# Where the first softmax of the second batch starts: its maxima moved one weight step earlier, its exponentials half a block earlier

## The chip, the cores and the metric

The kernel runs on one core of one Trainium2 chip. The metric is the device time of one execution in microseconds (us), lower is better. PE is TensorE (matrix products), DVE is VectorE, ACT is ScalarE, POOL is GpSimd, and SP issues the loads and stores.

## The reference, cut to what matters

Attention with two kinds of mask (four heads see the last 32 positions, four see every 32nd position) over 2 batches of 576 tokens, then a gated product of two linear layers with two more linear layers behind it, then four experts that are mixed by given probabilities.

```python
scores = scale * np.matmul(q, k.transpose(0, 1, 3, 2))      # B, H, S, D = 2, 8, 576, 64
scores = np.where(masks, scores, -1e9)
scores = scores - np.max(scores, axis=-1, keepdims=True)
attn = np.exp(scores); attn = attn / (np.sum(attn, axis=-1, keepdims=True) + 1e-09)
x = np.matmul(attn, v)                                       # to (1152, 512)
a = x @ w1; b = x @ w2; h = a * b @ w3; x = h @ w_out        # d_ff = 1024
for e in range(4):
    out += p[:, e:e + 1] * (np.maximum(x @ w1e[e], 0.0) @ w2e[e])
```

## The kernel before

Every matrix product with weights is made of three products of a value split in a high and a low part (`mm3`, lines 303 to 307). The weights arrive as 64-bit numbers and are turned into such pairs on the chip by a **worker**, a generator (`work`, lines 260 to 291). `advance(1)` makes its next step. For one chunk of weights the steps are `clamp` (DVE, L185), `shift` (DVE, L188), `round_up` and `sign` (ACT L144, DVE L191), then `magnitude` of the next chunk with `add` of this one (ACT L149, DVE L195), and, when the next chunk has begun, the split in the high part (ACT, L203) and the low part (DVE, L232). Product block `ft` needs both parts of chunk `ft`.

The order of all work is written out by hand: every engine runs its own instructions strictly in the order in which the program issues them. From line 1044 on, `run_unit` issues one **unit** after another: unit number `done` covers one `ft` and one half (288 tokens) of a batch. A unit has two half blocks of twelve matmuls each. The first ends in a copy of the accumulator by ACT (L609), the second in a product by DVE (L611) that reads the second accumulator and that copy. After each half block comes one step of the worker. Units 0 and 1 are made ahead of the loop, so the loop begins with unit 2.

Between the units the attention of the second batch is threaded in by `attend(1, s)`. Batch 1 has six chunks of scores. `attend` with s = 0 to 8 issues, among other things, the row maxima of chunk s (`maxima`: DVE reduction L409, then POOL multiplies the maxima by the negative scale, L411), the normalisation of chunk s-1 (POOL L436 adds a constant to the sums, DVE L453 takes reciprocals, DVE L457 multiplies), the transposes of chunk s-2 (PE, L462) and, from s = 2 on, the scores of chunk s+1 (PE, L396 and L403). The scores of chunks 0 to 2 are made ahead of the loop (line 1035). The exponentials of chunk s (`slots_exps`: ACT, L433, six or eight of them, one for each slot, each with its sum) are not issued by `attend`; it puts the chunk on the list `waiting`, and `run_unit` issues them at the end of the next half block, behind the worker's step there.

So before the change `attend(1, 0)` stands behind unit 3, `attend(1, 1)` behind unit 4 and `attend(1, 2)` behind unit 5. The exponentials of chunk 0 are issued at the end of the first half block of unit 4.

Of the kernel before, what the change touches and what calls it, by code (L numbers as in the profile page):

```python
# [44 lines left out]
def kernel(  # L45
# [249 lines left out]
    def advance(n=1):  # L295

        return all([next(worker, False) for _ in range(n)])

    def need(c, part=0):
        while not (c.done if part == 0 else c.done1 if part == 1 else c.done2):  # L300
            assert advance()
# [284 lines left out]
    def ab_block(b, ft, n):  # L586
        t = slice(b * S + n * HB, b * S + n * HB + HB)
        pair, late = ft // 2, b == 0 and ft < 6
        ab = tmp.tile([P, HB], F32, tag="pT", name="ab")
        if n == 0 and ft % 2 == 0:  # L590
            if late:
                if pair < 2:
                    parts = big[pair].tile([P, 2, 2, S], F32, tag="big", name="ab_f32")
                    whole[pair] = parts[:, 0]
                    if pair:
                        whole[2] = parts[:, 1]
            elif (b, pair) not in parts_of:
                ab_place(b, pair)
        if late:
            full = whole[pair][:, ft % 2, n * HB:n * HB + HB]  # L600
        else:
            full = ab
            pieces = ab_pieces(b, ft, n * HB, HB)
        for w in range(2):
            acc = bank("ab_acc")[:, :HB]
            for k in range(4):
                mm3(acc, c_w12[ft].parts((w * 4 + k) * P, P), (x_hi[:, k, t], x_lo[:, k, t]), k == 0, k == 3)
            if w == 0:
                nc.scalar.copy(ab, acc)  # L609
            else:  # L610
                nc.vector.tensor_tensor(out=full, in0=acc, in1=ab, op=ALU.mult)  # L611
            yield
        if late:
            return
        split_hi(pieces, ab)
        yield
        split_lo(pieces, ab)
        yield
# [241 lines left out]
    with tc.manual_schedule():  # L860
# [22 lines left out]
        done = 0  # L883
# [2 lines left out]

        waiting = []

        def run_unit():

            nonlocal done, rest
            b, ft, i = units[done]
            if done >= 2:
                need(c_w12[ft])
            block = ab_block(b, ft, i)
            for _ in range(2):
                next(rest, None)
                next(block)
                if done >= 2:
                    advance(1)  # L900
                if waiting:
                    waiting.pop().slots_exps()
            rest = block
            done += 1
            if b == i == 1:
                c_w12[ft].free()

        def attend(b, s):

            nonlocal live  # L910
            chunk = chunks[b]
            n = len(chunk)
            if 3 <= s + 1 < n:
                chunk[s + 1].scores()
            if s < n:
                chunk[s].maxima()
            if 1 <= s <= n:
                chunk[s - 1].recip()
                chunk[s - 1].normalise()
            if 3 <= s:  # L920
                c = chunk[s - 3]
                c.pv()
                c.put()
                c.put_lo()
                if c.g == 0:
                    live -= 1
            if 2 <= s < n + 2:
                chunk[s - 2].transposes()
                chunk[s - 2].evac(nc.scalar.copy)
            if s < n:  # L930
                waiting.append(chunk[s])
# [109 lines left out]
        done = 2  # L1041
        advance(4)
        steps = iter(range(9))
        while done < 16:
            if done == 3:
                need(c_w12[2])
            run_unit()
            if done in (4, 5, 6, 7, 8, 10, 11, 13, 14):
                attend(1, next(steps))
            if done == 6:  # L1050
                zero.whole_split()
        load_probs()
        while done < 32:
            run_unit()
            if done in (18, 21, 24):
                ab_split({18: 0, 21: 1, 24: 2}[done])
# [50 lines left out]
        for c in wc[:3]:  # L1107
# [6 lines left out]
        steps = [Step(half, e, c, c_e[16 * i + 4 * e + c])  # L1114
                 for i, half in enumerate(halves) for e in range(E) for c in range(4)]
# [100 lines left out]
```

## Time and profile before

| what | value |
|---|---|
| time, median of 3 runs | 616.2 us (616.09 to 616.81) |
| the profiled execution's own time | 618.54 us |
| its span, first to last instruction | 616.8 us |
| PE busy | 610.5 us (99%) |
| DVE busy | 442.1 us (72%) |
| ACT busy | 279.9 us (45%) |
| POOL busy | 16.2 us (3%) |
| mean granted TensorE clock | 0.997 |

The profiled execution took 618.54 us as a whole; its trace covers 616.8 us of that. A busy PE is one that has matmuls in flight. The share of an engine is a mean over stages of different kinds: the place of the change lies between 40 and 60 us, where DVE has much less room than its 72% say.

### The profile page before, as it was taken

The numbers are of one execution on the slowest core, as the hardware profiler recorded it, in microseconds if no ns is written. First come the engines' busy times: TensorE is split into PE (matmuls) and PEld (weight loads), VectorE is DVE, ScalarE is ACT, GpSimd is POOL, SyncE is SP. The second block draws the span as 40 slices with busy tenths as digits, with TensorE's granted clock in tenths as the row PEclk, the third lists the DMA queues.
The fourth block names the chain that finished last, engine by engine and source line by source line (L and its number), as shares of the span: only waits on it lengthen the run. The fifth ranks groups of instructions, "written<-read, shape, count | busy, mean of one in ns | idle before, by whom it ended". The sixth has DMA issues, their size and how long they took to land.

```text
span 616.8 us, 11164 instructions
## 1 busy us (share of the span) xinstructions
PE 610.5 (99%) x4488; PEld 557.0 (90%) x4488; DVE 442.1 (72%) x805; ACT 279.9 (45%) x562; POOL 16.2 (3%) x45
## 2 busy tenths in 40 slices
PE   8999999999999999999999999999999999999997
PEld 5789999998889999999899998999889898989996
DVE  4799977999753227777877987887766665755843
ACT  4769966776743134333343433434343333333320
POOL 4102200000000000000000000000000000000000
PEclk9899999999999999999999999999999999999999
DMA  8987340245412201333445344435585557464411
GB/s 264 319 299 210 135 143 2 82 157 201 176 68 94 85 28 69 137 138 136 192 158 193 121 158 168 167 144 205 184 324 196 214 193 249 162 234 175 153 53 69
DMA packets 28314, 99.48 MB, mean 161 GB/s; under 512 B 2630, under 2 KB 6158, under 8 KB 25830
## 3 DMA queue, kind: packets, MB, share of 16 engines
q1 hardware_dynamic: 27718, 98.17, 44.6%
q8 instruction: 35, 0.57, 0.4%
q10 hardware_dynamic: 544, 0.59, 0.3%
q14 instruction: 17, 0.14, 0.1%
HBM read 79.62 MB, written 19.14 MB: 160 GB/s over the span
## 4 chain that ended last, share of the span: by engine, by line
PE 98%; DMA 1%; issue 0%; ACT 0%; DVE 0%; ACTq 0%
PE g_acc L305 11%; PE g_acc L306 11%; PE g_acc L307 11%; PE ab_acc L305 5%; PE ab_acc L307 5%; PE ab_acc L306 5%; PE m_a L307 4%; PE m_a L306 4%; PE m_a L305 4%; PE m_b L306 3%; PE m_c L305 3%; PE m_b L305 3%; PE m_c L306 3%; PE x_acc L305 3%; PE m_c L307 3%; PE m_b L307 3%
## 5 line engine op out<-in xcount | busy, mean ns | idle before, releaser
L769 ACT ACTIVATE h_hi<-u 128x320 fp32r<-128x320 f32 (+1 forms) x128 | 56.9, 445 | 189.2 <-DVE u L775 189.2
L305 PE MATMUL g_acc<-w_hi,h_hi 128*128 128x512 f32 (+1 forms) x296 | 114.3, 386 | 0.0
L306 PE MATMUL g_acc<-w_lo,h_hi 128*128 128x512 f32 (+1 forms) x296 | 114.2, 386 | 0.0
L307 PE MATMUL g_acc<-w_hi,h_lo 128*128 128x512 f32 (+1 forms) x296 | 113.7, 384 | 0.0
L708 DVE TENSOR_TENSOR w_lo<-raw,w_hi 128x768 fp32r<-128x768 f32 x64 | 69.5, 1086 | 12.4 <-ACT w_hi L706 12.3
L775 DVE TENSOR_TENSOR u<-m_b,u 128x320 f32<-128x320 f32 (+1 forms) x96 | 40.8, 453 | 50.1 <-PE m_b L307 50.1
L305 PE MATMUL ab_acc<-x_hi,w_hi 128*128 128x288 f32 x240 | 71.4, 297 | 0.0
L307 PE MATMUL ab_acc<-x_hi,w_lo 128*128 128x288 f32 x240 | 70.7, 295 | 0.0
L306 PE MATMUL ab_acc<-x_lo,w_hi 128*128 128x288 f32 x240 | 70.7, 294 | 0.0
L307 PEld LDWEIGHTS g_acc<-w_hi,h_lo 128*128 128x128 f32 x296 | 55.6, 188 | 11.6
L305 PEld LDWEIGHTS g_acc<-w_hi,h_hi 128*128 128x128 f32 x296 | 55.8, 188 | 8.0
L306 PEld LDWEIGHTS g_acc<-w_lo,h_hi 128*128 128x128 f32 x296 | 55.8, 188 | 7.6
L771 DVE SCALAR_TENSOR_TENSOR h_lo<-u,h_hi 128x320 fp32r<-128x320 f32 (+1 forms) x128 | 57.9, 452 | 3.6 <-ACT h_hi L769 1.4
L706 ACT CAST w_hi<-raw 128x768 fp32r<-128x768 f32 x64 | 59.9, 936 | 0.0
L305 PEld LDWEIGHTS ab_acc<-x_hi,w_hi 128*128 128x128 f32 x240 | 45.0, 188 | 0.1
L306 PEld LDWEIGHTS ab_acc<-x_lo,w_hi 128*128 128x128 f32 x240 | 45.0, 188 | 0.0
L307 PEld LDWEIGHTS ab_acc<-x_hi,w_lo 128*128 128x128 f32 x240 | 45.0, 188 | 0.0
L306 PE MATMUL m_b<-b_t,s_hi 128*128 128x320 f32 (+1 forms) x128 | 37.9, 296 | 0.0
L775 DVE TENSOR_TENSOR u<-m_a,u 128x320 f32<-128x320 f32 (+1 forms) x64 | 28.9, 452 | 11.6 <-PE m_a L307 11.6
L708 DVE TENSOR_TENSOR s_lo<-raw,s_hi 128x1024 fp32r<-128x1024 f32 x16 | 19.6, 1226 | 24.3 <-ACT s_hi L706 24.3
L775 DVE TENSOR_TENSOR u<-m_c,u 128x320 f32<-128x320 f32 (+1 forms) x64 | 29.1, 454 | 4.5 <-PE m_c L307 3.9
L785 ACT COPY u<-m_a 128x320 f32<-128x320 f32 (+1 forms) x32 | 12.8, 399 | 42.1 <-PE m_a L307 42.1
(182 smaller groups left out, 1396.4 us busy)
## 6 DMA issues: line engine op xcount, KB each, us to landing
raw<-in_e_dram SPq DMA_DIRECT2D x32, 1024.0 KB, 4.9
raw<-in_w3T_dram SPq DMA_DIRECT2D x8, 1024.0 KB, 4.9
stored<-s_hi SPq DMA_DIRECT2D x16, 512.0 KB, 2.6
stored<-s_lo SPq DMA_DIRECT2D x16, 512.0 KB, 2.7
s_hi<-stored SPq DMA_DIRECT2D x16, 512.0 KB, 3.7
s_lo<-stored SPq DMA_DIRECT2D x16, 512.0 KB, 5.4
raw<-in_w_dram SPq DMA_DIRECT2D x7, 1024.0 KB, 7.8
raw<-in_w_out_dram SPq DMA_DIRECT2D x4, 1024.0 KB, 5.0
```

Of the source, the lines that this page charges most:

```text
L305: mm(acc, lh, rh, start=first, stop=False)
L306: mm(acc, lh, rl, start=False, stop=False)
L307: mm(acc, ll, rh, start=False, stop=last)
L706: nc.scalar.copy(dst[0], src)
L708: nc.vector.tensor_tensor(out=dst[1], in0=src, in1=dst[0].bitcast(F32), op=ALU.subtract)
L769: nc.scalar.activation(hi, src, AF.Relu)
L771: nc.vector.scalar_tensor_tensor(out=lo, in0=src, scalar=0.0, in1=hi.bitcast(F32), op0=ALU.max, op1=ALU.subtract)
L775: nc.vector.tensor_tensor(out=out, in0=acc, in1=b, op=ALU.add)
L785: nc.scalar.copy(u1, a)
```

## The change

`run_unit` takes a function that it calls in the second half block of the unit, behind the block's own instructions and ahead of the worker's step. It is given for unit 3 alone, and does `attend(1, 0)` there; the call behind unit 3 is gone. The list of the other eight calls is as it was.

```diff
-        def run_unit():
+        def run_unit(between=None):
...
-            for _ in range(2):
+            for i_half in range(2):
                 next(rest, None)
                 next(block)
+                if between and i_half:
+                    between()
                 if done >= 2:
                     advance(1)
                 if waiting:
...
+        def begin():
+            attend(1, next(steps))
+
         while done < 16:
             if done == 3:
                 need(c_w12[2])
-            run_unit()
-            if done in (4, 5, 6, 7, 8, 10, 11, 13, 14):
+            run_unit(begin if done == 3 else None)
+            if done in (5, 6, 7, 8, 10, 11, 13, 14):
                 attend(1, next(steps))
```

`attend(1, 0)` issues the maxima of chunk 0 and puts the chunk on `waiting`. Since the list is looked at behind the worker's step of the same half block, the exponentials move too.

On DVE, from the worker's `sign` step in unit 3 on, these rows stood before (`raw` and `t` are a chunk of weights, `ab_f_623` the products of units 2 and 3, `ab_f_831` those of unit 4, `mx` the maxima, `sc` the scores):

```order
L191 SCALAR_TENSOR_TENSOR t<-raw_611,t 128x1024
L611 TENSOR_TENSOR ab_f_623<-ab_acc,ab 128x288
L195 ISA t<-raw_611,t 128x2048
L409 TENSOR_REDUCE mx<-sc 128x6
L185 TENSOR_SCALAR t<-t 128x1024
L611 TENSOR_TENSOR ab_f_831<-ab_acc,ab 128x288
L232 TENSOR_TENSOR w_lo<-t,w_hi 128x1024
```

With the change the same place reads as follows (`ab_f_839` is the tile that was `ab_f_831`):

```order
L611 TENSOR_TENSOR ab_f_623<-ab_acc,ab 128x288
L409 TENSOR_REDUCE mx<-sc 128x6
L195 ISA t<-raw_611,t 128x2048
L185 TENSOR_SCALAR t<-t 128x1024
L611 TENSOR_TENSOR ab_f_839<-ab_acc,ab 128x288
```

The reduction L409 has changed places with the worker's addition L195; nothing else on DVE moved.

On ACT the difference between before (-) and the change (+) is this, from the worker's steps in unit 3 to those in unit 5 (the first L609 is the copy of unit 4, the second that of unit 5; `w_hi` is the high part of weight chunk 3; `p_ring` takes the exponentials):

```order
 L144 ACTIVATE raw_611<-raw_611 128x1024
 L149 ACTIVATE t<-raw_729 128x1024
-L609 COPY ab<-ab_acc 128x288
-L203 CAST w_hi<-t 128x1024
 L433 ACTIVATE p_ring,rec<-sc,mx 128x64 x6
+L609 COPY ab<-ab_acc 128x288
+L203 CAST w_hi<-t 128x1024
 L609 COPY ab<-ab_acc 128x288
 L144 ACTIVATE raw_729<-raw_729 128x1024
```

The six exponentials of chunk 0 now stand ahead of unit 4's copy and of the split of weight chunk 3. PE, POOL and SP issue the same instructions in the same order as before.

## Rows read from the trace of the kernel before

**Rows 1.** The page, part 1: engine, busy time, share of the span, instructions.

```profile
PE 610.5 (99%) x4488; PEld 557.0 (90%) x4488; DVE 442.1 (72%) x805; ACT 279.9 (45%) x562; POOL 16.2 (3%) x45
```

**Rows 2.** Waits of PE: us in total, times, longest us; first of four rows.

```profile
PE o L483 <- issue: 1.4, 1, 1.4
...
```

**Rows 3.** Timeline of PE, 49.5 to 51.3 us: start, duration, line, tiles, count.

```profile
49.51 0.34 PE L396 MATMUL sc<-m_str,i_str 128*128 128x432 bf16 x1
49.78 1.01 PE L403 MATMUL sc<-tqk 64*54 64x54 f32 x32
50.74 0.55 PE L462 MATMUL tp<-ident,p_ring 128*128 128x128 f32 x3
```

**Rows 4.** Timeline of DVE, 44.7 to 50.7 us.

```profile
44.77 0.45 DVE L611 TENSOR_TENSOR ab_f<-ab_acc,ab 128x288 f32<-128x288 f32 x1
45.14 1.22 DVE L195 CUSTOM_DVE_ANT_0 t<-raw,t 128x2048 uint16<-128x2048 uint16 x1
46.27 0.55 DVE L409 TENSOR_REDUCE mx<-sc 128x6 f32<-128x384 f32 x1
46.74 0.68 DVE L185 TENSOR_SCALAR t<-t 128x1024 f32<-128x1024 f32 x1
47.34 0.45 DVE L611 TENSOR_TENSOR ab_f<-ab_acc,ab 128x288 f32<-128x288 f32 x1
47.71 1.22 DVE L232 TENSOR_TENSOR w_lo<-t,w_hi 128x1024 fp32r<-128x1024 f32 x1
48.84 0.69 DVE L188 TENSOR_SCALAR t<-t 128x1024 int32<-128x1024 int32 x1
49.44 0.55 DVE L409 TENSOR_REDUCE mx<-sc 128x6 f32<-128x384 f32 x1
...
50.12 0.56 DVE L457 TENSOR_TENSOR p_ring<-p_ring,rec 128x384 f32<-128x384 f32 x1
```

**Rows 5.** Timeline of ACT, 43 to 50.9 us; in brackets the idle time before.

```profile
43.06 1.15 ACT L149 ACTIVATE t<-raw 128x1024 f32<-128x1024 f32 x1
44.89 0.40 ACT L609 COPY ab<-ab_acc 128x288 f32<-128x288 f32 x1 [0.68 <-PE ab_acc L307]
46.39 1.05 ACT L203 CAST w_hi<-t 128x1024 fp32r<-128x1024 f32 x1 [1.10 <-DVE t L195]
47.57 0.32 ACT L433 ACTIVATE p_ring<-sc,mx 128x64 f32<-128x64 f32 x1
...
49.33 0.42 ACT L609 COPY ab<-ab_acc 128x288 f32<-128x288 f32 x1
49.61 1.20 ACT L144 ACTIVATE raw<-raw 128x1024 int32<-128x1024 uint32 x1
```

**Rows 6.** Timeline of POOL, 46 to 59 us.

```profile
46.91 0.62 POOL L411 TENSOR_SCALAR mx<-mx 128x6 f32<-128x6 f32 x1 [27.01 <-DVE mx L409]
...
50.08 0.25 POOL L411 TENSOR_SCALAR mx<-mx 128x6 f32<-128x6 f32 x1 [0.21 <-DVE mx L409]
...
58.10 0.82 POOL L436 TENSOR_SCALAR rec<-rec 128x6 f32<-128x6 f32 x1 [3.99 <-ACT p_ring L433]
```

**Rows 7.** Timeline of DVE, 57 to 58.9 us, while that last POOL instruction ran.

```profile
57.05 1.22 DVE L232 TENSOR_TENSOR w_lo<-t,w_hi 128x1024 fp32r<-128x1024 f32 x1
58.19 0.69 DVE L188 TENSOR_SCALAR t<-t 128x1024 int32<-128x1024 int32 x1
```

**Rows 8.** Stretches: length, busy us and instructions by engine, granted clock (PEclk), DMA share, GB/s.

```profile
16.90:20.30 3.40, 2.01 (x88) 1.69 (x80) 2.62 (x7) 1.89 (x5) 2.09 (x6) 1.00 0.92 272
20.30:23.70 3.40, 3.40 (x56) 3.01 (x49) 1.46 (x3) 1.54 (x5) 0.00 (x0) 0.50 0.84 335
23.70:27.00 3.30, 3.19 (x74) 2.54 (x73) 2.58 (x5) 3.01 (x13) 0.00 (x0) 1.00 1.08 430
```

**Rows 9.** Timelines of SP and of ACT: a weight load, and the first reader of its data.

```profile
46.38 7.31 SPq L140 DMA_DIRECT2D raw<-in_w_dram  x2
...
62.07 1.37 ACT L149 ACTIVATE t<-raw 128x1024 f32<-128x1024 f32 x1
```

## The prediction, made before the change was run

> **What bounds the kernel now.** I read the page first: PE is busy for 610.5 of 616.8 us [rows 1]. A busy share can hide waits, so the waits of PE come next: there are four rows of them, 3.0 us in all, the longest 1.4 us [rows 2], and all lie in the first 20 us. Behind those PE waits for nothing the profile can show. That fixes what a change of order between 40 and 60 us can do: PE runs the same instructions in the same order, there is no wait to remove, so the time can only stay or grow by waits that are made new. The question is how much room each thing has that PE waits for.
>
> The timeline of PE shows where the room is smallest. Behind the matmuls of unit 5 come the scores of chunk 3 at 49.51 and 49.78, and at 50.74 the transposes of chunk 0 [rows 3]. The scores reuse the accumulator that the exponentials of chunk 0 read; the last of these is over shortly before the next ACT instruction at 49.33 [rows 5], so this one is met with almost no room, but it is met. The transposes need DVE's normalisation of chunk 0, which runs from 50.12 to 50.68 [rows 4]; the transposes start 0.06 us later [rows 3]. So **DVE may not be late here at all**: whatever it loses ahead of 50.12, PE loses at 50.74. Its rows from 44.77 on follow each other without a gap (none carries a wait) [rows 4]; DVE has no slack to lose it from.
>
> ACT, on the other hand, stands idle twice just there: 0.68 us ahead of unit 4's copy at 44.89 and 1.10 us ahead of the cast at 46.39 [rows 5]. The six exponentials take from 47.57 to 49.33, 1.76 us [rows 5]. They would just fill these two gaps, if their maxima were there in time.
>
> **When the maxima are there.** DVE's product of unit 3 starts at 44.77 and lets the next one start at 45.14 [rows 4]. So the reduction of chunk 0 starts at 45.14 instead of 46.27 and ends 0.55 us later, at 45.69. The addition L195 starts 0.47 us behind the reduction's start (before, L185 followed it so, 46.27 to 46.74 [rows 4]), at 45.61, and ends at 46.83. L185 follows 1.13 us behind it (45.14 to 46.27), at 46.74, as before, and ends at 47.42.
>
> The maxima then pass through POOL, which is not among the rows that moved but decides the case. Undisturbed its multiplication takes 0.25 us (at 50.08); at 46.91 it took 0.62 us and ended at 47.53, 0.11 us behind the end of DVE's L185 at 47.42 [rows 4, 6]. At 58.10 a POOL instruction of the same size began while DVE ran L232, which ended at 58.27; L188 had started at 58.19, ahead of that end, and POOL was done at 58.92, just behind L188's end at 58.88 [rows 6, 7]. So POOL is held by some DVE instructions, and when the next such one starts before the first has ended, it is held through both. That is the new case: POOL starts 0.09 us behind the reduction (46.91 less 46.82), at 45.78, when L195 already runs, and L195 runs into L185. Held through both it ends at about 47.5, where it ended before. The exponentials then start at 47.57 as before: **earlier in the order, not in time**. POOL has nothing else queued until the sums.
>
> The Trainium skill, "SBUF — State Buffer", section "SBUF: two separate sides", says that GpSimd and some VectorE instructions share a pair of ports as an exclusive lock, which whoever starts first has for its whole instruction. The holding at 46.91 agrees with it. It does not say who has the lock when POOL has waited through L195 and L185 started before that was over; if POOL has it, the sum is that of the second rival.
>
> **What is queued behind them now.** Before, ACT did unit 4's copy at 44.89 and the cast of weight chunk 3 at 46.39, ahead of the exponentials. Now both wait behind them, and DVE waits for both:
>
> - The exponentials end at 47.57 + 1.76 = 49.33. The copy follows, 49.33 to 49.75 (0.42, as the copy there took [rows 5]).
> - DVE's product of unit 4 needs the copy: it starts at 49.79 instead of 47.34 [rows 4].
> - The cast starts 0.28 us behind the copy (49.33 to 49.61 [rows 5]), at 49.61, takes 1.05 to 1.1, ends at about 50.68.
> - DVE's low part L232 needs the cast: it starts at 50.72 instead of 47.71. **DVE is 3.0 us late.**
> - The spacings stay: L188 1.13 behind L232, the reduction of chunk 1 at 0.60 behind that, the normalisation 0.68 behind that (47.71, 48.84, 49.44, 50.12 [rows 4]). It runs from 53.13 to 53.69, and the transposes start at 53.75 instead of 50.74.
>
> So PE stands still for **3.0 us**, behind its scores. The lower bound of this cost is with POOL not held at all (0.25 us): exponentials at 46.06, copy at 47.82, cast to 49.16, L232 at 49.20, 1.5 us late.
>
> Nothing else is lost by it. The weight load on SP that started at 46.38, right behind L195's end (46.36), now starts 0.47 us later; its data have their first reader at 62.07 [rows 9], over 8 us after the row's end. ACT's copy of unit 5 goes from 49.33 to about 50.6, late by less than PE. Behind the transposes PE, DVE and ACT are all late by 2.7 to 3.0 us, so no new wait follows; and as PE had no waits later, nothing gives the 3.0 us back. The gain is the 0.04 us at most by which the scores at 49.51 may have waited.
>
> **The clock.** A pause of PE can cost a second time. Between 16.9 and 20.3 us PE was busy for 2.01 of 3.40 us, in it the longest wait; behind this, from 20.3 to 23.7 us, the granted clock was 0.50, that is 1.2 GHz, and 1.00 (2.4 GHz) from then on [rows 8]. In 3.4 us at half clock PE does 1.7 us less work. The new pause makes PE less busy than that stretch: from 50.8 to 54.2 us it would work for about 0.5 us. Against a fall speaks that PE runs dense matmuls in the units ahead of the new pause, but had only small ones ahead of the old. I take it as likelier than not that the clock falls once: 1.7 us; bounds 0 and 1.7. At half clock PE and not DVE limits, so the two costs add.
>
> **Sum**, against the profiled execution: span 616.8 + 3.0 + 1.7 = 621.5 us, its own time 618.5 + 4.7 = 623.2. The median of the runs is 2.3 below the profiled time, 616.2; the same sum gives 620.9.
>
> **Rivals.**
> - *The pause without the clock's fall*: 616.2 + 3.0 = 619.2 us. Its condition is above.
> - *POOL is let in early*: between L195 and L185, at about 46.95, the exponentials start at 47.0 and DVE is 2.45 us late: 618.7, or 620.4 with the clock's fall; never held, 1.5 us: 617.7. Against it speaks 58.10, where the change of instruction did not let POOL in.
> - *Not slower: the exponentials fill ACT's gaps.* For this they must end by the time at which ACT had the cast to do, 46.39: a start at 44.6. For a loss under 1.23 us (0.2%, about what a measurement of this kernel tells from no change) DVE may be that late, so the exponentials must start by 45.8. The reduction ends at 45.69 and POOL adds 0.34 at best; DVE would have to be some 0.3 us ahead of this trace in the timed runs, with POOL free. Then 616.2 to 617.4.
> - *More than one fall or a second pause* (POOL held again for chunk 1, say): 1 to 2 us more, 622.5.
>
> **How the numbers follow.** Pause and fall 0.47; pause alone 0.27; POOL early 0.16; not slower 0.05; more 0.05. The prediction is the likeliest, 620.9. The range from 618.4 to 621.5 leaves out the last two and the half of "POOL early" that is under 618.4, 0.2 at most. Slower by over 0.2% (617.4) is every case but one: 0.94; same 0.04, faster 0.02, since the trace shows no wait of PE to remove.
>
> **What would show it.** In the profile of the change: the first POOL multiplication at about 45.8 with a long duration (1.7 us); exponentials still at about 47.6; a wait of DVE's L611 for ACT's copy of 2.4 us and of L232 for the cast of 0.5; a new wait of PE at the transposes L462 for DVE's L457 of about 3 us, from 50.8 to 53.7; PEclk at 0.5 for some 3.4 us behind it. It is wrong if the transposes start before 51.5, or if another wait of PE is longer than this one.

## The result, and the profile after

The change takes 621.37 us (median of 6 runs, 618.71 to 622.97), the kernel before 616.78 (6 runs, 616.09 to 617.18). The ratio is 1.0069 with a 95% interval of 1.0052 to 1.0085: **slower by 0.7%**, some 4.3 us. Forecast were 620.9 us and a range from 618.4 to 621.5. The profiled execution has a span of 621.2 us, where that of before had 616.8. It is the longest of the six runs of the change, as the profiled one of before was longer than its median.

The waits of PE in the changed kernel (us in total, times, longest), beside [rows 2]:

```profile
PE tp L462 <- DVE p_ring L457: 2.9, 1, 2.9
PE idle L120 <- DVE idle L112: 1.0, 1, 1.0
PE o L483 <- issue: 0.8, 1, 0.8
```

The first row is new: the transposes of chunk 0 wait for DVE's normalisation. The timeline of PE there, which answers to [rows 3] (in brackets the idle time before, and what ended it):

```profile
49.43 0.36 PE L396 MATMUL sc<-m_str,i_str 128*128 128x432 bf16 x1
49.72 1.01 PE L403 MATMUL sc<-tqk 64*54 64x54 f32 x32
53.64 0.55 PE L462 MATMUL tp<-ident,p_ring 128*128 128x128 f32 x3 [2.91 <-DVE p_ring L457]
```

The scores come as before, the transposes at 53.64 instead of 50.74. DVE, which answers to [rows 4]:

```profile
44.72 0.45 DVE L611 TENSOR_TENSOR ab_f<-ab_acc,ab 128x288 f32<-128x288 f32 x1
45.09 0.55 DVE L409 TENSOR_REDUCE mx<-sc 128x6 f32<-128x384 f32 x1
45.55 1.22 DVE L195 CUSTOM_DVE_ANT_0 t<-raw,t 128x2048 uint16<-128x2048 uint16 x1
46.68 0.69 DVE L185 TENSOR_SCALAR t<-t 128x1024 f32<-128x1024 f32 x1
49.65 0.46 DVE L611 TENSOR_TENSOR ab_f<-ab_acc,ab 128x288 f32<-128x288 f32 x1 [2.29 <-ACT ab L609]
50.60 1.22 DVE L232 TENSOR_TENSOR w_lo<-t,w_hi 128x1024 fp32r<-128x1024 f32 x1 [0.49 <-ACT w_hi L203]
...
53.02 0.56 DVE L457 TENSOR_TENSOR p_ring<-p_ring,rec 128x384 f32<-128x384 f32 x1
```

The reduction did move ahead, by 1.2 us. But behind L185 DVE now stands 2.29 us for ACT's copy and 0.49 us for ACT's cast; before, neither row had a wait. The normalisation comes 2.9 us later, and PE with it. Why the copy is late stands in the rows of POOL and ACT, which answer to [rows 5, 6]:

```profile
45.72 1.69 POOL L411 TENSOR_SCALAR mx<-mx 128x6 f32<-128x6 f32 x1 [25.15 <-DVE mx L409]
```

```profile
43.00 1.20 ACT L149 ACTIVATE t<-raw 128x1024 f32<-128x1024 f32 x1
47.44 0.31 ACT L433 ACTIVATE p_ring<-sc,mx 128x64 f32<-128x64 f32 x1 [3.24 <-POOL mx L411]
...
49.20 0.42 ACT L609 COPY ab<-ab_acc 128x288 f32<-128x288 f32 x1
49.48 1.09 ACT L203 CAST w_hi<-t 128x1024 fp32r<-128x1024 f32 x1
```

POOL got the maxima at 45.72 and was done at 47.41, just behind the end of DVE's L185 (46.68 + 0.69 = 47.37): it was held through L195 and L185. So the exponentials started at 47.44, where they had started at 47.57 [rows 5]; ACT stood 3.24 us ahead of them, with the copy (before at 44.89) and the cast (before at 46.39) queued behind.

Then the clock, in stretches of the changed kernel (the columns are those of [rows 8]):

```profile
51.00:54.40 3.40, 0.76 (x6) 0.77 (x7) 3.37 (x6) 2.04 (x9) 0.25 (x1) 1.00 0.27 99
54.40:57.80 3.40, 3.40 (x17) 3.40 (x16) 3.19 (x7) 3.40 (x11) 1.26 (x2) 0.51 0.22 34
57.80:61.20 3.40, 3.40 (x94) 3.09 (x94) 3.40 (x5) 3.21 (x16) 0.49 (x1) 0.99 0.87 341
```

Behind the stretch in which PE was busy for 0.76 of 3.40 us the granted clock is at half (1.2 GHz) for about 3.4 us, and then at 2.4 GHz again. Pause and half clock make 2.9 + 1.7 = 4.6 us; the spans differ by 4.4. The early stretch at half clock, from 20.3 to 23.7 us, is in both profiled executions (granted clock 0.50 there in both), so that the difference does not come from it.

### The profile page after: what moved, and what is told of

Read it like the earlier page. It is cut to its first block, busy times and chain, and to the rows that moved or that the text cites. A ratio compares the mean times of both kernels' runs of the same rounds, so it can differ in the third digit from the quotient of the medians.

```text
span 621.2 us, 11164 instructions
## 1 busy us (share of the span) xinstructions
PE 612.1 (99%) x4488; PEld 558.6 (90%) x4488; DVE 442.7 (71%) x805; ACT 280.2 (45%) x562; POOL 17.3 (3%) x45
## 3 DMA queue, kind: packets, MB, share of 16 engines
q1 hardware_dynamic: 27718, 98.17, 44.7%
## 4 chain that ended last, share of the span: by engine, by line
PE 94%; DVE 2%; ACT 1%; DMA 1%; issue 1%; POOL 0%; DVEq 0%; ACTq 0%
PE g_acc L305 11%; PE g_acc L306 11%; PE g_acc L307 11%; PE ab_acc L305 5%; PE ab_acc L306 5%; PE ab_acc L307 5%; PE m_a L307 4%; PE m_a L306 4%; PE m_a L305 4%; PE m_b L306 3%; PE m_c L305 3%; PE m_c L306 3%; PE m_b L305 3%; PE x_acc L305 3%; PE m_c L307 3%; PE m_b L307 3%
```

## The experiments

The theory: the exponentials stand ahead of the copy and the cast but cannot start sooner, because POOL is held; so DVE waits for the copy, PE for DVE, and the clock falls in the pause. The rivals: the swap on DVE itself is the cost; the place of the exponentials costs whenever the maxima come; the half clock is free.

**One half at a time.** First the maxima moved and the exponentials left where they were:

```diff
-                if waiting:
+                if waiting and not (between and i_half):
```

> The maxima of chunk 0 ahead of the worker's addition as in the change, the exponentials where they stood before (behind unit 4's copy and the cast). Theory (the exponentials ahead of copy and cast cost the pause): POOL is held to about 47.5 as in the change, but copy and cast do not wait for it. The addition is 0.47 us later, so the cast runs 46.9 to 47.9, the exponentials to about 49.7, and the scores and transposes are late by 0.25 to 0.4 us; no fall of the clock; 0.2 to 0.5 us over before, about 617.1. Rival (the change of places on DVE, with POOL held for 1.7 us, is the cost): the whole pause of 2.9 us, 619.7 to 621.4.

Measured: 617.32 us (12 runs) against 617.53 (23 runs of before on the same chip), ratio 0.9993 (0.9979 to 1.0007): no difference that the times show. The whole pause, 2.9 us or 0.5%, lies far outside the interval. In its trace POOL is held just as long:

```profile
44.06 1.69 POOL L411 TENSOR_SCALAR mx<-mx 128x6 f32<-128x6 f32 x1 [23.37 <-DVE mx L409]
```

but the copy and the cast run ahead of the exponentials, and PE has no wait for DVE's normalisation. The lateness forecast is there in small: the scores start 0.40 us behind the last matmul of unit 5, where before they had started 0.17 behind it (49.34 to 49.51). First the row of before, then the two with the maxima moved:

```profile
49.34 0.29 PE L307 MATMUL ab_acc<-x_hi,w_lo 128*128 128x288 f32 x1
```

```profile
47.62 0.29 PE L307 MATMUL ab_acc<-x_hi,w_lo 128*128 128x288 f32 x1
48.02 0.34 PE L396 MATMUL sc<-m_str,i_str 128*128 128x432 bf16 x1
```

So the swap on DVE and POOL's long hold cost nothing that could be timed. The other half, the exponentials moved and the maxima left behind the worker's addition:

```diff
-                if between and i_half:
-                    between()
                 if done >= 2:
                     advance(1)
+                if between and i_half:
+                    between()
                 if waiting:
```

> The maxima behind the worker's addition as before, the exponentials ahead of unit 4's copy and the cast as in the change. Theory: POOL ends at 47.5 and the exponentials start at 47.6 either way, so the copy starts at about 49.3 and the pause at the transposes is 2.9 to 3.0 us, with the clock's fall 4.6: like the change, about 621.4. Rival (the change of places on DVE is the cost): as before, 616.8.

Measured: 622.01 us, ratio 1.0064 (1.0040 to 1.0088), like the whole change. The pause, in its timeline of PE:

```profile
53.81 0.47 PE L462 MATMUL tp<-ident,p_ring 128*128 128x128 f32 x1 [2.98 <-DVE p_ring L457]
```

**With the maxima as late as here, the place of the exponentials is the whole cost**; that the maxima came 1.2 us sooner in the change gave nothing. Whether that place costs by itself, or only because the maxima are late for it, these two kernels do not tell.

**When the maxima are ready.** Three kernels keep the exponentials' new place and have the multiplied maxima ready sooner. (In a kernel to which lines were added, later lines have higher numbers: L434 is L433 of the change, L610 its L609.) In the first, ACT multiplies chunk 0's maxima, as it does for the first batch, and POOL does not:

```diff
-            if self.b:
+            self.by_act = not self.b or self.index == 0
+            if not self.by_act:
                 nc.gpsimd.tensor_scalar_mul(mx[:, :s], mx[:, :s], -SCALE)
...
-            if not self.b:
+            if self.by_act:
                 nc.scalar.activation(self.mx[:, :self.slots], ...
```

> The change, but chunk 0's maxima are multiplied by ACT ahead of the exponentials, not by POOL. Theory: POOL's hold through two DVE instructions sets the start of the exponentials. Without it they start at about 46.0 instead of 47.4, the copy at 47.7, and the pause at the transposes is 1.4 us instead of 2.9; with half the pause the clock may or may not fall: 618.2, or 619.9 with a fall. Rival (the exponentials would not start sooner anyway, or the pause is set by something else): pause 2.9 us, about 621.4.

Measured: 618.55 us against 617.53, ratio 1.0014 (1.0001 to 1.0027). The pause is 1.6 us (1.4 expected), and no fall of the clock behind it shows (granted clock 0.999 or 1.0 in all 12 runs). In the second, the maxima are issued ahead of unit 3:

```diff
+            if done == 3:
+                begin()
             run_unit(begin if done == 3 else None)
```

(in `run_unit` the call of `between` is gone, and the exponentials are kept back to the end of the second half block.)

> The exponentials as in the change, but the maxima of chunk 0 a whole unit earlier, ahead of unit 3. Theory (what costs is that the maxima come too late for the place of the exponentials): the reduction runs at 43.5, POOL is held by the worker's DVE instruction of 1.2 us to about 45.4, the exponentials run from 45.5 to 47.2, the copy starts at 47.2, the cast ends at 48.6, DVE is 0.9 us late and the pause 0.9 us, without a fall of the clock: about 617.7. Rival (exponentials ahead of the copy and the cast cost by their place in the order, whenever the maxima come): pause 2.9 us, 619.7 to 621.4.

Measured: 618.06 us against 616.95, ratio 1.0015 (1.0000 to 1.0030), pause 1.0 us. The third does both:

> As the kernel with the maxima ahead of unit 3, and ACT multiplies them. Theory: the multiplication runs at about 44.1, the exponentials from 44.4 to 46.1, in the idle time that ACT had before; copy at 46.1, cast at 46.9 because the addition is 0.47 us later; DVE 0.25 us late, pause at most 0.3 us: 616.8 to 617.1, no different from before. It cannot be faster, since PE had no wait there. Rival (the place in the order costs): 619 to 621.

Measured: 618.38 us against 616.95, ratio 1.0012 (0.9994 to 1.0030), by the interval not to be told from before. The median is above the 616.8 to 617.1 that was expected, and the times do not set this kernel below the second one; three of its twelve runs (619.43 to 620.79) have a granted clock of 0.993 to 0.997, as three of the 23 of before have one of 0.991 to 0.994. The rival's 619 to 621 lies outside the interval, which ends at 618.8. What the kernel does, its trace says better than its time. Here the exponentials run in ACT's gaps and the copy has no wait to give to DVE:

```profile
42.64 0.21 ACT L431 ACTIVATE mx<-mx 128x6 f32<-128x6 f32 x1
42.88 0.31 ACT L434 ACTIVATE p_ring<-sc,mx 128x64 f32<-128x64 f32 x1
...
44.63 0.43 ACT L610 COPY ab<-ab_acc 128x288 f32<-128x288 f32 x1
45.27 1.06 ACT L203 CAST w_hi<-t 128x1024 fp32r<-128x1024 f32 x1 [0.22 <-DVE t L195]
```

The transposes' waits in the traces of the three, in this order; in the third none is listed:

```profile
50.06 0.55 PE L463 MATMUL tp<-ident,p_ring 128*128 128x128 f32 x3 [1.61 <-DVE p_ring L458]
```

```profile
50.59 0.55 PE L462 MATMUL tp<-ident,p_ring 128*128 128x128 f32 x3 [0.98 <-DVE p_ring L457]
```

The start of the exponentials in the first two of them (that of the third, 42.88, is above):

```profile
43.86 0.31 ACT L434 ACTIVATE p_ring<-sc,mx 128x64 f32<-128x64 f32 x1
```

```profile
44.40 0.31 ACT L433 ACTIVATE p_ring<-sc,mx 128x64 f32<-128x64 f32 x1 [1.15 <-POOL mx L411]
```

Counted from the start of unit 5's last matmul, the exponentials start 1.86 us ahead of it in the change, 3.16 in the first of the three, 3.78 in the second and 5.01 in the third (the times are in the table below). That is 1.30, 1.92 and 3.15 us sooner than in the change, and the pause of 2.91 us becomes 1.61, 0.98 and none: what the exponentials gain comes off the pause one for one, as the theory has it. The rival that the place costs by itself falls.

**The clock.** Matmuls without use, between the scores and the transposes, keep PE at work in the pause:

```diff
             self.tp = bank("tp")[:, :self.frames * P]
+            if self.b and self.index == 0:
+                for _ in range(8):
+                    mm(self.tp.rearrange("p (a b) -> p a b", a=3), ident,
+                       ident.unsqueeze(1).to_broadcast([P, 3, P]), start=True, stop=True)
```

> The change, and in the pause, between the scores of chunk 3 and the transposes of chunk 0, eight matmuls of 128x384 in 32-bit floats into the transposes' accumulator, whose results are overwritten; about 2.6 us of work that is in nobody's way. Theory (the clock's fall behind the pause is the other 1.7 us of the loss): transposes as late as in the change, at about 53.6, no stretch of half clock behind them, 1.7 us less than the change: about 619.7. Rival (behind the pause DVE and ACT limit, and the half clock costs nothing): the clock stays up and the time is that of the change, about 621.4.

Measured: 622.16 us, ratio 1.0081 (1.0054 to 1.0108). This tells nothing between the two, since the filling was too long:

```profile
52.01 0.36 PE L396 MATMUL sc<-m_str,i_str 128*128 128x432 bf16 x1
53.23 5.43 PE L463 MATMUL tp<-ident 128*128 128x384 f32 x16
58.49 0.49 PE L466 MATMUL tp<-ident,p_ring 128*128 128x128 f32 x3
```

The eight stand as sixteen in the trace and took 5.3 us. The transposes came 6.5 us behind the start of the scores, 2.3 later than in the change (49.43 to 53.64). With four, and the change itself beside it:

> The kernel that filled the pause, with four matmuls of 128x384 instead of eight: the eight ran as sixteen of 0.325 us and took 5.2 us, more than the pause; four take 2.6 us and fit in it. Theory (the clock's fall behind the pause costs 1.7 us on top of the pause): transposes as late as in the change, 2.9 us, no stretch of half clock behind them, every run at a granted clock of 0.999 to 1.0 unless it falls in the first 30 us; about 2.5 to 2.9 us over before and some 1.7 us under the change run beside it. Rival (behind the pause DVE and ACT limit, the half clock is free): the clock stays up and the time is that of the change.

> The change once more, beside the kernel that fills the pause. Theory: the pause of 2.9 us in every run; the clock's fall behind it in most of them, readable in the granted clock (0.999 without, 0.996 to 0.997 with one fall), and the runs with a fall 1.7 to 2 us longer than those without; median 4 to 4.7 us over before. Rival: time and granted clock do not go together.

Measured: 620.23 us (618.98 to 620.62) for the filled pause, ratio 1.0047 (1.0029 to 1.0065), by which it is 2.9 us over before; 622.12 us (620.61 to 622.93) for the change, ratio 1.0077 (1.0058 to 1.0096). The filled one has a granted clock of 1.0 in all six runs, the change 0.995 to 0.997 in all six. In the filled one the transposes start right behind DVE's normalisation (51.73 + 0.56 = 52.29), so the chain of lateness is the same:

```profile
51.73 0.56 DVE L457 TENSOR_TENSOR p_ring<-p_ring,rec 128x384 f32<-128x384 f32 x1
```

```profile
49.35 2.85 PE L463 MATMUL tp<-ident 128*128 128x384 f32 x8
52.35 0.55 PE L466 MATMUL tp<-ident,p_ring 128*128 128x128 f32 x3
```

and the stretches behind it, of the filled kernel and of the change, differ in the clock:

```profile
51.00:55.00 4.00, 3.85 (x25) 3.04 (x24) 3.97 (x8) 3.04 (x14) 1.25 (x2) 1.00 0.05 18
```

```profile
51.00:55.00 4.00, 3.76 (x17) 3.76 (x18) 3.94 (x7) 4.00 (x16) 1.27 (x2) 0.57 0.15 20
```

The half clock is not free: 622.12 - 620.23 = 1.9 us between two medians of six runs, which spread over 1.6 and 2.3 us; half speed over 3.4 us makes 1.7. That runs of the change with a fall are longer than those without, the other expectation, could not be read in the repetition, since all six have a low granted clock. In the first six the two at 0.999 are the two shortest.

**The same without the start.** Much of the spread of whole runs arises ahead of the change: unit 5's last matmul starts between 46.89 and 51.87 us in the ten traces. From it to DVE's last sum is the part that the change can touch. The two rows of before, of the change in the repetition, and of the four matmuls:

```profile
49.34 0.29 PE L307 MATMUL ab_acc<-x_hi,w_lo 128*128 128x288 f32 x1
613.63 0.48 DVE L841 SCALAR_TENSOR_TENSOR sum<-g_acc,pn,sum 128x256 f32<-128x256 f32 x1 [0.23 <-PE g_acc L307]
```

```profile
46.89 0.29 PE L307 MATMUL ab_acc<-x_hi,w_lo 128*128 128x288 f32 x1
615.68 0.48 DVE L841 SCALAR_TENSOR_TENSOR sum<-g_acc,pn,sum 128x256 f32<-128x256 f32 x1 [0.23 <-PE g_acc L307]
```

```profile
47.99 0.29 PE L307 MATMUL ab_acc<-x_hi,w_lo 128*128 128x288 f32 x1
615.23 0.48 DVE L845 SCALAR_TENSOR_TENSOR sum<-g_acc,pn,sum 128x256 f32<-128x256 f32 x1 [0.23 <-PE g_acc L307]
```

The starts of the three rows in all ten traces, with the wait at the transposes of chunk 0 (us):

| kernel | exponentials of chunk 0 | unit 5's last matmul | wait | last sum | from matmul to sum, over before |
|---|---|---|---|---|---|
| before | 47.57 | 49.34 | none | 613.63 | 0 (564.29) |
| maxima moved alone | 46.10 | 47.62 | none | 612.16 | 0.25 |
| exponentials moved alone | 47.62 | 49.17 | 2.98 | 618.16 | 4.70 |
| the change | 47.44 | 49.30 | 2.91 | 618.07 | 4.48 |
| the change, repeated | 45.05 | 46.89 | 2.92 | 615.68 | 4.50 |
| ACT multiplies | 43.86 | 47.02 | 1.61 | 612.94 | 1.63 |
| maxima ahead of unit 3 | 44.40 | 48.18 | 0.98 | 613.48 | 1.01 |
| both | 42.88 | 47.89 | none | 612.29 | 0.11 |
| pause filled with eight | 49.91 | 51.87 | filled | 621.33 | 5.17 |
| pause filled with four | 46.16 | 47.99 | filled | 615.23 | 2.95 |

Where the clock does not fall, the kernel loses what its pause is long (1.63 for 1.61, 1.01 for 0.98, 2.95 for the filled one). With a fall it loses 4.50 - 2.95 = 1.5 us more. That is the price of the half clock free of the start's spread, one trace against one. As whole runs these two traces differ by only 0.4 us (618.8 and 618.4), since in that of the change unit 5's last matmul started 1.1 us sooner.

## Why the prediction was right

- *PE had nothing to gain.* Right. The version without a pause (the third of the three) is not faster than before either.
- *POOL is held through L195 and L185.* Right: begun at 45.72 (45.78 forecast), done at 47.41 (about 47.5). The rival "POOL is let in early" falls: the change from one holding instruction to the next did not let it in. That the hold decides the size was shown by taking POOL out: 1.3 us less pause. By itself it costs little: with the maxima moved alone POOL is held as long.
- *Copy and cast queue behind the exponentials, DVE behind them.* Right in place and size: DVE's waits 2.29 and 0.49 us; L232 at 50.60 (50.72 forecast). The experiment with the exponentials alone gives the whole cost, the one with the maxima alone none.
- *The pause at the transposes*, 3.0 us forecast: 2.9. No second pause followed, and none of it came back: with the clock held up the kernel is 2.9 us over before, by its ratio and in its trace.
- *The clock's fall*, put at 0.47 against 0.27 for the pause without it: in the change's first six runs the granted clock is 0.999 in two (618.71 and 619.96 us) and 0.994 to 0.997 in four (621.26 to 622.97), in the repetition 0.995 to 0.997 in all six. Both cases exist, the fall is the commoner. A low granted clock alone does not say where the clock fell: 7 of the 57 runs of before that were timed beside the experiments have one under 0.999 too. But the two traces of the change show the fall behind the pause. Its price was 1.5 us in the traces and 1.9 by the medians, 1.7 forecast.
- *The range.* The median is 0.13 us under its upper end, and that it lies inside is in part luck: over a third of the sum, the fall, does not come in every run. By their granted clock two of the first six had none; in the repetition, where all six have a low granted clock, the median is 622.12, over that end, with before at 616.97. Single runs reach 622.97; that one is the profiled run, which has the early fall besides.

The rivals "not slower" and "a second pause" fall with the same rows. The point that "not slower" named, exponentials that fit in ACT's gaps, is what the kernel with early maxima and ACT's multiplication does; it comes out level with before as far as its times tell (0.1 us over it in the trace), as the lack of any wait of PE said.

## What to carry to other kernels

On an engine that runs its instructions in the order of issue, as ACT did here, an instruction that is moved ahead does not start sooner if its input does not come sooner; it only makes what it overtook wait as well (here 3.24 us of ACT standing idle). Before moving one, follow its input through every engine, the small POOL step between two large ones included, and read which later instruction of the overtaken ones has the least room. Where the busiest engine shows no wait in the stretch, a change in the order of the others has nothing to win and can cost, and a pause on TensorE can cost again by the clock (here 2.9 us, then 1.5 more). Where the start of a kernel varies more than the effect, compare traces from one instruction behind the start to the end.

## What the runs showed of the hardware

- The same POOL instruction on 128x6 numbers took 0.25 us alone [rows 6] and 1.69 us where two DVE instructions that hold it followed each other.
- A pause of 2.9 to 3.0 us in dense matmuls was followed by half clock (1.2 GHz) in all three traces that have it, two of the change and one of the exponentials moved alone. A low granted clock (0.994 to 0.997) is in 15 of the 18 runs of these kernels, against 7 of 57 runs of before. In the kernel whose pause is 1.6 us every one of 12 runs has a granted clock of 0.999 or 1.0.
- In one execution (the first filled kernel) the early fall came too, and lasted longer than that of before [rows 8], though PE was busy all the time:

```profile
16.10:19.50 3.40, 2.56 (x85) 2.03 (x78) 3.11 (x9) 2.27 (x7) 2.03 (x5) 1.00 0.89 293
19.60:29.80 10.20, 10.20 (x161) 8.48 (x158) 6.48 (x12) 7.45 (x19) 0.93 (x2) 0.50 0.95 334
```

  Of the 23 runs of before beside it, three have a granted clock under 0.999 (618.86, 620.16 and 620.24 us, median of all 617.53). They have no trace, so that it was the early fall is only argued; what makes it come in one run and not in the next stays open.
